# A sliding-window attention and MLP kernel: rows of maxima sent by ScalarE, and four of six feature blocks made 512 tokens at a time

## The chip, the cores and the metric

One NeuronCore of a Trainium2 chip runs the whole kernel; the others are idle. The metric is the device time of one execution in microseconds, the median of several runs. A profiled execution gives the trace that the profile is made from. The engines are named as the profile names them: PE is TensorE, ACT ScalarE, DVE VectorE, POOL GpSimd, SP SyncE.

## The reference

2048 tokens of 640 features are layer-normalised. One branch is attention with 32 heads of 20 features over a window of 256 tokens; the other is an MLP with 1536 hidden features and a squared ReLU. The output gates one with the other.

```python
xn = _layernorm(x)
# attention, H = 32, Dh = 20, W = 256
qkv = (xn @ wqkv).reshape(B, S, 3, H, Dh)
scores = einsum("bhqd,bhkd->bhqk", q, k) * Dh ** -0.5
scores = where(0 <= q_index - k_index < W, scores, -1e9)
s = (softmax(scores) @ v).reshape(B, S, D) @ wo
# MLP, D = 640, F = 1536
h = xn @ w1 + b1
r = where(h > 0, h, 0)
g = silu((r * r) @ w2 + b2)
out = x + s * g
```

## The kernel before

**Precision.** Each large product is made three times: an operand is split into a high part (rounded) and a low part (the rest), and high x high, high x low and low x high are added up in PSUM. ACT makes the high part, DVE or POOL subtracts it to get the low part. So one feature block of the first MLP half, with 5 chunks of 128 input features, takes 15 products.

**Half products.** The fillers below run each product as two halves of 64 contraction rows (`half`, L466). The front half of a job runs in one stream, its back half some time later in a second stream (`ahead`, `behind`, `backlog`), and the two streams alternate on PE, so that two halves of different jobs are on the array together. PE takes its instructions strictly in the order in which they were written: a product that waits for something holds both streams.

**Stages.** A first stage (to about 116 us) normalises, transposes and makes V and the first group of Q and K. A last one (from about 804 us) multiplies by `wo` and gates. Between them run 267 steps of attention, one query block of 128 tokens of a pair of heads each, and between the instructions of each step `fill` puts filler work: the other groups of Q and K (`qkps`), then the MLP, in eight blocks: two halves of the hidden features (`hf`), each over four blocks of 512 tokens (`b`).

**A step of attention.** `scores` writes the scores of one query block (`sps`), `maxima` takes their row maxima on DVE. Nine steps later (`LAG`) `scores_t` makes the transposed scores (`stps`), with two more contraction rows: ones on one side, the negative maxima (high and low part) on the other. `exps` takes the exponential on ACT into `p`, POOL cuts the window's corners, and `values` multiplies by V once in four steps (`ops`). One pair of banks holds `stps`, so the next `scores_t` waits until the exponential has read the last one.

Every fourth step `max_rows` (L488) turns the maxima of four query blocks: PE transposes, ACT negates and copies (`row`, L499), ACT rounds (`mrow`, L500), POOL subtracts (L501), and two DMAs (L503) on SP's queue bring the two rows, 4 KB each, into the two spare rows of `qs`. The `stps` that reads them first comes three steps after they are issued.

**A block of the MLP** (L891 on). Its first half makes hidden features: the loop `for th in range(2): for fp in range(NFH // 2)` (L912) goes over two token halves of 256 and three pairs of feature blocks, six accumulations. Each (`Acc`, one of three PSUM banks of 512 columns) holds two feature blocks of the same 256 tokens, 30 products of 256 columns. Its evacuation has two passes, `part(0)` and `part(1)`, one for each feature block: ACT `relu` and `hh` (the square, rounded), DVE `sq` (the exact square), POOL `hl` (the low part). The second pass is put 0.8 us of planned time later by `later`; when its POOL instruction is written, the accumulation counts as `made` and its bank as free 1.0 us on.

The second half makes 4 token tiles (`tt`) x 2 output halves (`nh`), jobs of 18 products of 320 columns (`yps`), three for each of six feature blocks (`fc`); their weights are slices of `hh` and `hl`. A product waits in the plan, `while (tt // 2, fc // 2) not in made`, and tiles 0 and 1 need only the accumulations of the first token half.

**What sets the order.** The order is written out ahead of time by this planner (`COST`, `pace`, `later`, `room`), engine by engine; on the chip only the waits on semaphores move it.

Of the kernel before, what the change touches and what calls it, by code (L numbers as in the profile page):

```python
# [9 lines left out]
F32 = mybir.dt.float32  # L10
# [19 lines left out]
HP = P // 2  # L30
HALF = D // 2
NFH = F // 2 // P
FHALF = F // 2
MT = 256
LAG = 9
# [17 lines left out]
def f32(ap):  # L53
    return ap.bitcast(F32)
# [3 lines left out]
def attn_mlp_kernel(ctx: ExitStack, tc, x, wqkv, wo, w1, b1, w2, b2, out):  # L58
# [429 lines left out]
    def max_rows(p, g, tps):  # L488
        i = p % 2

        def one(j):
            r = slice(j * HP, (j + 1) * HP)
            nc.tensor.transpose(tps[:HP, j, 3 * P:3 * P + HP], mts[g % 2][r, :], ident[r, r])
        both(lambda: one(0), lambda: one(1), COST[P])

        def rest():
            row = at2.tile([8, P], F32, tag="row", bufs=1, name="row")
            mrow = at2.tile([8, 2, P], F32R, tag="mrow", bufs=1, name="mrow")
            nc.scalar.activation(row.rearrange("m (j n) -> m j n", j=2), tps[:8, :, 3 * P:3 * P + HP], AF.Copy, scale=-1.0)  # L499
            nc.scalar.activation(mrow[:, 0, :], row, AF.Copy)  # L500
            nc.gpsimd.tensor_sub(mrow[:, 1, :], row, f32(mrow[:, 0, :]))  # L501
            for a in range(2):
                nc.sync.dma_start(f32(qs[i])[KR + a:KR + a + HP + 1:HP, g * BT:(g + 1) * BT].rearrange("h (q n) -> h q n", q=4), f32(mrow)[:, a, :])  # L503
        return rest

    pts = {}
# [319 lines left out]
    def filler():  # L826
# [64 lines left out]
        for n, (hf, b) in enumerate(blocks):  # L891
# [13 lines left out]
            def used(n=n, b=b, nxt=nxt):  # L905
# [3 lines left out]
                    shut.discard("o")  # L909
                if n < last and blocks[n + 1][1] != b:  # L910
                    nxt.extend(load_xb(blocks[n + 1][1]))
            for th in range(2):  # L912
                for fp in range(NFH // 2):
                    yield from room()
                    ps = Acc(BT, "hps")

                    def evac(ps=ps, th=th, fp=fp, fi=hf * NFH + 2 * fp, hs=hs, made=made):
                        hh = [stg.tile([P, BT], F32R, tag="stg", name="hh"),
                              stg.tile([P, BT], F32R, tag="stg", name="hl") if fp == 0 else wgt.tile([P, D], F32R, tag=f"wg{'kq'[fp % 2]}l", name="hl")[:, :BT]]
                        hs[th, fp] = hh  # L920

                        def part(i):
                            vload[0] += 0.5
                            sl = slice(i * MT, (i + 1) * MT)
                            r = at2.tile([P, MT], F32, tag="relu", name="relu")
                            nc.scalar.activation(r, ps.tile[:, sl], AF.Relu, bias=b1t[:, fi + i:fi + i + 1])  # L926
                            nc.scalar.activation(hh[0][:, sl], r, AF.Square)

                            def rest():
                                sq = at2.tile([P, MT], F32, tag="sq", name="sq")  # L930
                                nc.vector.scalar_tensor_tensor(sq, ps.tile[:, sl], b1t[:, fi + i:fi + i + 1], r, ALU.add, ALU.mult)  # L931
                                nc.gpsimd.tensor_sub(hh[1][:, sl], sq, f32(hh[0][:, sl]))  # L932
                                if i:
                                    made.add((th, fp))
                                    ps.free(1.0)
                            later(0.7, rest)
                        part(0)
                        later(0.8, lambda: part(1))
                    job = open_job(evac, *([used] if (th, fp) == (1, NFH // 2 - 1) else []))
                    mms = [(i, lin1(wt1, (wp * KC + c) * FHALF + (2 * fp + i) * P, P), xb[xp][:, c * BT + th * MT:c * BT + (th + 1) * MT]) for i in range(2) for c in range(KC) for wp, xp in ((0, 0), (0, 1), (1, 0))]  # L940
                    for m, (i, w_, x_) in enumerate(mms):
                        halves(job, ps, w_, x_, m == 0, m == len(mms) - 1, i * MT, MT)
                        yield 0.1065
            if n % NB == 0:
                ensure(f"2{hf}")
            if n == NB:
# [3 lines left out]
            for tt in range(4):  # L950
                t = b * 4 + tt
                place = [None]
                jobs = []

                def start(nh, hf=hf, t=t, place=place, idx=4 * (n - NB) + tt, end=n == NB - 1 and tt == 3, n=n, tt=tt):
                    sl = slice(nh * HALF, (nh + 1) * HALF)
                    ps = Acc(HALF, "yps")

                    def evac():
                        vload[0] += 0.5  # L960
                        if not nh:
# [12 lines left out]

                def product(jb, nh, fc):
                    ps, job, _ = jb
                    while (tt // 2, fc // 2) not in made:
                        if state[2] < 10 ** 6:
                            yield None
                        elif tasks:  # L980
                            finish()
                        else:
                            drain(backlog, 1)
                    for hp, wp in ((0, 0), (0, 1), (1, 0)):
                        jb[2] += 1
                        halves(job, ps, hs[tt // 2, fc // 2][hp][:, fc % 2 * MT + tt % 2 * P:fc % 2 * MT + (tt % 2 + 1) * P], lin1(wt2, (wp * NFH + fc) * D + nh * HALF, HALF), jb[2] == 1, jb[2] == 3 * NFH)
# [117 lines left out]
    whole = [False]  # L1104
    fl = filler()
    steps = NP * NT + LAG + PLAG
    pace = (8 * (KC - 1) * 15 * COST[BT] + 4 * NB * (3 * 30 * COST[MT] + 4 * 18 * COST[HALF]) + NP * (2 * NT * COST[3 * P] + NB * PV)) / (steps - 1)

    def fill(upto):
        soon()  # L1110
# [89 lines left out]
```

## Time and profile before

| what | value |
|---|---|
| median of 3 runs | 885.0 us (881.82 to 885.83) |
| the profiled execution | 882.05 us, of which the traced span is 880.3 |
| granted TensorE clock, mean | 0.999 |
| DVE, ACT, POOL busy | 57%, 47%, 37% of the span |
| data moved | 168.59 MB, mean 192 GB/s |

The profile gives the busy time of each engine, the waits ("who waited for whom", total, times and longest), and the chain of work that ended last, followed back from the end. A group line gives engine, operation, output and inputs by the program's names, shapes, count, then busy time, the mean of one in ns, and the idle time before them. A line of the timeline gives the start and the length in us. "64*128" is the number of contraction rows and output columns of the array that a product uses. Matmuls overlap each other, so the length of one (283 ns) is not what it costs; the distance between two is.

### The profile page before, as it was taken

To read this page: it belongs to the slowest core of one execution; us is meant where nothing else is said; L and a number is where in the kernel's file an instruction comes from. 1 tells how busy PE (TensorE), PEld (TensorE's weight loads), DVE (VectorE), ACT (ScalarE), POOL (GpSimd) and SP (SyncE) were. 2 spreads that over 40 slices of the span, in tenths; PEclk is the share of its full clock that TensorE was granted. 3 is DMA by queue.
4 is the path that set the end of the run, shared out by engine and by line. 5 is a ranking of instruction groups with operands and counts; after the bars stand their busy time and mean duration, and the time that the engine had idled before them with its cause. 6 is when DMAs were issued, how large, how long until landed. Compare 5 with 4: busy or idle time off the path is not lost.

```text
span 880.3 us, 26692 instructions
## 1 busy us (share of the span) xinstructions
PE 860.6 (98%) x10640; PEld 802.6 (91%) x10640; DVE 498.7 (57%) x1448; ACT 414.8 (47%) x800; POOL 329.9 (37%) x700
## 2 busy tenths in 40 slices
PE   8999999999999999999999999999999999999997
PEld 8999999888888899989989989988998989989997
DVE  7652146656567755555555676754655555354774
ACT  5222114545556744744644664743653654642231
POOL 6010002333333643534633543643543543621343
PEclk9999999999999999999999999999999999999999
DMA  7997687778788363263366255475255364165995
GB/s 269 313 394 265 179 230 256 229 249 278 240 269 297 84 223 108 60 224 96 95 207 174 73 154 145 130 223 150 76 202 161 90 209 119 52 196 183 284 299 175
DMA packets 85988, 168.59 MB, mean 192 GB/s; under 512 B 8680, under 2 KB 40552, under 8 KB 83304
## 3 DMA queue, kind: packets, MB, share of 16 engines
q1 hardware_dynamic: 85864, 166.89, 60.1%
q8 instruction: 84, 1.38, 0.7%
q14 instruction: 40, 0.33, 0.1%
HBM read 94.71 MB, written 71.57 MB: 189 GB/s over the span
## 4 chain that ended last, share of the span: by engine, by line
PE 76%; DMA 11%; ACT 4%; DVE 4%; issue 3%; POOL 2%; SPq 0%; DVEq 0%; POOLq 0%; ACTq 0%
PE yps L468 16%; PE hps L468 16%; PE qkps L468 13%; PE ops L546 8%; PE vps L228 8%; DMA qs<-mrow 5%; PE stps L518 4%; PE sps L478 4%; PE qkps L205 3%; DMA out_dram<-res 3%; POOL res L1099 2%; PE wops L599 1%; DMA ks<-k_d 1%; ACT p L524 1%; ACT relu L926 1%
## 5 line engine op out<-in xcount | busy, mean ns | idle before, releaser
L486 DVE CUSTOM_DVE_ANT_0 junk<-sps,mask 128x384 bf16<-128x384 f32 (+2 forms) x512 | 271.9, 531 | 205.0 <-PE sps L478 75.1
L524 ACT ACTIVATE p<-stps 128x768 f32<-128x768 f32 (+2 forms) x256 | 196.9, 769 | 258.0 <-PE stps L518 202.1
L468 PE MATMUL yps<-w,hh 64*128 64x320 f32 x1536 | 231.6, 310 | 4.0 <-DVE sq L931 3.0
L525 POOL TENSOR_SCALAR_AFFINE_SELECT p<-p 128x256 f32<-128x256 f32 x256 | 104.6, 409 | 332.7 <-ACT p L524 327.6
L468 PE MATMUL hps<-xb,w 64*128 64x256 f32 x2520 | 218.2, 283 | 0.0
L468 PEld LDWEIGHTS hps<-xb,w 64*128 64x128 f32 x2520 | 206.4, 187 | 5.2 <-issue 5.1
L468 PEld LDWEIGHTS yps<-w,hh 64*128 64x128 f32 x1536 | 188.8, 185 | 9.7 <-DVE sq L931 4.8
L468 PE MATMUL yps<-w,hl 64*128 64x320 f32 x768 | 182.8, 309 | 0.0
L478 PE MATMUL sps<-ks,qs 60*128 60x384 f32 (+2 forms) x512 | 139.9, 344 | 1.9 <-DVE mt L486 1.6
L518 PE MATMUL stps<-qs,ks 62*128 62x384 f32 (+2 forms) x512 | 130.1, 335 | 5.8 <-DMA qs<-mrow 5.7
L468 PEld LDWEIGHTS yps<-w,hl 64*128 64x128 f32 x768 | 121.6, 185 | 2.1 <-issue 2.1
L468 PE MATMUL qkps<-xT,wgkh 64*128 64x512 f32 x320 | 100.9, 395 | 0.0
L468 PE MATMUL qkps<-xT,wgqh 64*128 64x512 f32 x320 | 99.4, 393 | 0.0
L546 PE MATMUL ops<-p,vp 128*21 128x128 f32 (+1 forms) x2112 | 92.8, 313 | 0.0
L527 POOL TENSOR_SCALAR_AFFINE_SELECT p<-p 128x256 f32<-128x256 f32 x224 | 92.1, 411 | 0.0
L518 PEld LDWEIGHTS stps<-qs,ks 62*128 62x128 f32 x512 | 83.4, 187 | 8.7 <-issue 7.7
L478 PEld LDWEIGHTS sps<-ks,qs 60*128 60x128 f32 x512 | 84.4, 185 | 5.1 <-DVE mt L486 3.9
L546 PEld LDWEIGHTS ops<-p,vp 128*21 128x21 f32 x2112 | 65.2, 100 | 22.3 <-issue 8.8
L932 POOL TENSOR_TENSOR hl<-sq,hh 128x256 fp32r<-128x256 f32 x96 | 70.6, 736 | 27.5 <-DVE sq L931 22.9
L228 PE MATMUL vps<-wv,xT 128*128 128x320 f32 x480 | 71.5, 308 | 0.0
L228 PEld LDWEIGHTS vps<-wv,xT 128*128 128x128 f32 x480 | 70.5, 188 | 0.1
L931 DVE SCALAR_TENSOR_TENSOR sq<-hps,b1t,relu 128x256 f32<-128x256 f32 x96 | 46.2, 482 | 39.2 <-ACT relu L926 39.1
(100 smaller groups left out, 1212.1 us busy)
## 6 DMA issues: line engine op xcount, KB each, us to landing
ks<-k_d SPq DMA_DIRECT2D x64, 240.0 KB
qs<-q_d SPq DMA_DIRECT2D x64, 240.0 KB
xb<-xs SPq DMA_DIRECT2D x12, 1280.0 KB
xs<-xT SPq DMA_DIRECT2D x8, 1280.0 KB
y<-ysb SPq DMA_DIRECT2D x32, 320.0 KB
k_d<-shm SPq DMA_DIRECT2D x19, 512.0 KB
q_d<-shm SPq DMA_DIRECT2D x19, 512.0 KB
o<-osb SPq DMA_DIRECT2D x64, 128.0 KB
```

The source lines that it names most:

```text
L205: nc.tensor.matmul(ps, wt[:, c, :], xT[part][b][:, c * BT + t0:c * BT + t0 + n], start=m == 1, stop=m == 3 * KC)
L228: nc.tensor.matmul(ps, xT[xp][b][:, c * BT + t * P: c * BT + (t + 1) * P], wv[wp][:, c, nh * HALF:(nh + 1) * HALF], start=first and m == 0 ...
L468: return nc.tensor.matmul(out, a[r], b_[r], skip_group_check=True, **kw)
L478: nc.tensor.matmul(ss[hh][:, :nk], qs[i][o, q * P:(q + 1) * P], ks[i][o, k0 * P:k0 * P + nk], start=True, stop=True)
L486: nc.vector.tensor_tensor_reduce(out=junk[:, :nk], in0=ss[hh][:, :nk], in1=mask[:, 3 * P - nk:], scale=1.0, scalar=-3.0e38, op0=ALU.add, o ...
L518: nc.tensor.matmul(tps[:, hh, :n], ks[i][o, kb * P:(kb + 1) * P], qs[i][o, kb * P:kb * P + n], start=True, stop=True)
L524: nc.scalar.activation(p32[:, :, :n], tps[:, :, :n], AF.Exp, scale=SCALE)
L525: nc.gpsimd.affine_select(p32[:, :, 0:P], p32[:, :, 0:P], pattern=[[0, 2], [1, P]], compare_op=ALU.is_ge, fill=0.0, base=0, channel_multip ...
L527: nc.gpsimd.affine_select(p32[:, :, 2 * P:], p32[:, :, 2 * P:], pattern=[[0, 2], [-1, P]], compare_op=ALU.is_gt, fill=0.0, base=0, channel ...
L546: nc.tensor.matmul(ot[r0:r0 + VW, c0:c0 + len(part), :], vps[p][:, kb // 4, kb % 4, hh, :], pt[:, hh, :].rearrange("p (t n) -> p t n", n=P ...
L931: nc.vector.scalar_tensor_tensor(sq, ps.tile[:, sl], b1t[:, fi + i:fi + i + 1], r, ALU.add, ALU.mult)
L932: nc.gpsimd.tensor_sub(hh[1][:, sl], sq, f32(hh[0][:, sl]))
```

## The change

Two things. `max_rows` issues its two DMAs on ScalarE's queue instead of SP's, the first at once, the second 0.8 us of planned time later. And the first half of an MLP block makes feature blocks 0 to 3 (`WIDE = NFH - 2`) with all 512 tokens, one block to a bank, 15 products of 512 columns and one evacuation of 512 columns; blocks 4 and 5 stay as before: two accumulations, one for each token half, with two blocks of 256 tokens. The second half finds its slices accordingly, and `pace` follows from the new costs.

```diff
@@ max_rows
-            for a in range(2):
-                nc.sync.dma_start(f32(qs[i])[KR + a:KR + a + HP + 1:HP, g * BT:(g + 1) * BT].rearrange("h (q n) -> h q n", q=4), f32(mrow)[:, a, :])
+            def send(a):
+                nc.scalar.dma_start(f32(qs[i])[KR + a:KR + a + HP + 1:HP, g * BT:(g + 1) * BT].rearrange("h (q n) -> h q n", q=4), f32(mrow)[:, a, :])
+            send(0)
+            later(0.8, lambda: send(1))
@@ filler, first half of a block
-            for th in range(2):
-                for fp in range(NFH // 2):
-                    ps = Acc(BT, "hps")
+            for u in range(NFH):
+                ps = Acc(BT, "hps")
+                th = u - WIDE
+                cols = [(u, 0, BT)] if th < 0 else [(WIDE + i, th * MT, MT) for i in range(2)]
...
-                            later(0.7, rest)
-                        part(0)
-                        later(0.8, lambda: part(1))
+                        later(0.7, rest)
+                    part(0)
+                    if len(cols) > 1:
+                        later(0.8, lambda: part(1))
...
-                    mms = [(i, lin1(wt1, (wp * KC + c) * FHALF + (2 * fp + i) * P, P), xb[xp][:, c * BT + th * MT:c * BT + (th + 1) * MT]) for i in range(2) for c in range(KC) for wp, xp in ((0, 0), (0, 1), (1, 0))]
+                mms = [(i, lin1(wt1, (wp * KC + c) * FHALF + fc * P, P), xb[xp][:, c * BT + t0:c * BT + t0 + n_]) for i, (fc, t0, n_) in enumerate(cols) for c in range(KC) for wp, xp in ((0, 0), (0, 1), (1, 0))]
@@ second half of a block
-                    while (tt // 2, fc // 2) not in made:
+                    u = fc if fc < WIDE else WIDE + tt // 2
+                    o = tt * P if fc < WIDE else (fc - WIDE) * MT + tt % 2 * P
+                    while u not in made:
```

Two places of the written order. The first is PE's order in the fourth MLP block, at the end of the first `yps` job (its 13th to 18th products) while the sixth accumulation's back half runs beside it. "waits" names the engine whose semaphore the instruction stands for. Before, where the weights `hh_8552` and `hl_8553` are the third accumulation's:

```order
L468 MATMUL yps_8781<-w2_0_1_3933,hh_8552 128x320
L468 MATMUL hps_8673<-xb0_2_7524,w1_0_1_3364 128x256
L468 MATMUL yps_8781<-w2_0_2_4087,hh_8552 128x320
L468 MATMUL hps_8673<-xb0_2_7524,w1_0_0_3362 128x256
L468 MATMUL yps_8781<-w2_0_1_3933,hl_8553 128x320
L468 MATMUL hps_8673<-xb1_2_7525,w1_0_0_3362 128x256
L468 MATMUL yps_8894<-w2_0_0_3931,hh_8284 128x320 [waits DVE_49]
```

With the change, where `hh_8268` and `hl_8269` are the fifth accumulation's:

```order
L469 MATMUL yps_8262<-w2_0_1_3878,hh_8268 128x320 [waits Activation_49]
L469 MATMUL hps_8121<-xb0_2_7133,w1_0_1_3356 128x256
L469 MATMUL yps_8262<-w2_0_2_4007,hh_8268 128x320
L469 MATMUL hps_8121<-xb1_2_7134,w1_0_1_3356 128x256
L469 MATMUL yps_8262<-w2_0_1_3878,hl_8269 128x320 [waits Pool_49]
L469 MATMUL hps_8121<-xb0_2_7133,w1_0_2_3490 128x256
L469 MATMUL yps_8262<-w2_0_1_3878,hh_8268 128x320 [waits Activation_49]
L469 MATMUL hps_8121<-xb0_2_7133,w1_0_0_3354 128x256
L469 MATMUL yps_8262<-w2_0_2_4007,hh_8268 128x320
L469 MATMUL hps_8121<-xb1_2_7134,w1_0_0_3354 128x256
L469 MATMUL hps_8121<-xb0_2_7133,w1_0_1_3356 128x256
L469 MATMUL yps_8262<-w2_0_1_3878,hl_8269 128x320 [waits Pool_49]
```

The same products stand there, but they now wait for the two passes of the accumulation that was finished last.

The second place is ACT's order at the same point: the exponential (`p32`), the rows of maxima, and the two evacuation passes of the fifth accumulation (`hps_8525` before, `hps_8025` after). Before:

```order
L524 ACTIVATE p32_8815<-stps_8808 128x768
L551 ACTIVATE osb_8819<-ops_1358 128x256
L926 ACTIVATE relu_8824<-hps_8525,b1t_108 128x256
L927 ACTIVATE hh_8822<-relu_8824 128x256
L926 ACTIVATE relu_8842<-hps_8525,b1t_108 128x256
L927 ACTIVATE hh_8822<-relu_8842 128x256
L524 ACTIVATE p32_8878<-stps_8869 128x768
L499 ACTIVATE row_8882<-stps_8869 8x128
L500 ACTIVATE mrow_8883<-row_8882 8x128
```

With the change:

```order
L528 ACTIVATE p32_8249<-stps_8240 128x768
L500 ACTIVATE row_8253<-stps_8240 8x128
L501 ACTIVATE mrow_8254<-row_8253 8x128
L505 DMA qs1_1350<-mrow_8254 2x4x128
L933 ACTIVATE relu_8270<-hps_8025,b1t_108 128x256
L934 ACTIVATE hh_8268<-relu_8270 128x256
L505 DMA qs1_1350<-mrow_8254 2x4x128
L933 ACTIVATE relu_8291<-hps_8025,b1t_108 128x256
L934 ACTIVATE hh_8268<-relu_8291 128x256
L528 ACTIVATE p32_8315<-stps_8308 128x768
```

The two DMA issues are new on ACT; here one stands ahead of the first pass and one between the two passes.

More of the change, by code (lines that the diff above doesn't have):

```diff
@@ L32 @@
 NFH = F // 2 // P
+WIDE = NFH - 2
 FHALF = F // 2
@@ L911, in used @@
                     nxt.extend(load_xb(blocks[n + 1][1]))
-            for th in range(2):
-                for fp in range(NFH // 2):
-                    yield from room()
-                    ps = Acc(BT, "hps")
[L917 to L935, printed above, removed]
-                            later(0.7, rest)
-                        part(0)
-                        later(0.8, lambda: part(1))
-                    job = open_job(evac, *([used] if (th, fp) == (1, NFH // 2 - 1) else []))
-                    mms = [(i, lin1(wt1, (wp * KC + c) * FHALF + (2 * fp + i) * P, P), xb[xp][:, c * BT + th * MT:c * BT + (th + 1) * MT]) for i in range(2) for c in range(KC) for wp, xp in ((0, 0), (0, 1), (1, 0))]
-                    for m, (i, w_, x_) in enumerate(mms):
-                        halves(job, ps, w_, x_, m == 0, m == len(mms) - 1, i * MT, MT)
-                        yield 0.1065
@@ L985, in product @@
                         jb[2] += 1
-                        halves(job, ps, hs[tt // 2, fc // 2][hp][:, fc % 2 * MT + tt % 2 * P:fc % 2 * MT + (tt % 2 + 1) * P], lin1(wt2, (wp * NFH + fc) * D + nh * HALF, HALF), jb[2] == 1, jb[2] == 3 * NFH)
+                        halves(job, ps, hs[u][hp][:, o:o + P], lin1(wt2, (wp * NFH + fc) * D + nh * HALF, HALF), jb[2] == 1, jb[2] == 3 * NFH)
                         yield 0.133
```

26 lines of the change are left out of this document (25 added, 1 removed).

## The prediction

> **What bounds the kernel now.** First the page: the span, the engines, the chain by line.
>
> ```profile
> span 880.3 us, 26692 instructions
> PE 860.6 (98%) x10640; PEld 802.6 (91%) x10640; DVE 498.7 (57%) x1448; ACT 414.8 (47%) x800; POOL 329.9 (37%) x700
> q1 hardware_dynamic: 85864, 166.89, 60.1%
> ```
>
> TensorE (PE) is busy nearly throughout, so time goes only if PE needs less for its products or stands still less. ScalarE (ACT) is free half of the time. All transfers share one queue, which keeps the 16 DMA engines busy for 60% of the span. Next the view of waits, to see for what PE stands still and what SyncE's queue is held by:
>
> ```profile
> PE stps L518 <- DMA qs<-mrow: 5.7, 8, 1.7
> PE yps L468 <- DVE sq L931: 3.0, 6, 0.7
> SPq L503 <- ACT mrow L500: 66.2, 42, 3.2
> ACT p L524 <- PE stps L518: 202.1, 154, 4.0
> ```
>
> Two waits of PE matter here: eight times the transposed scores (`stps`) stand for the row of maxima that a DMA brings (5.7 us), and six times a second-half product (`yps`) stands for a bank that VectorE's `sq` still reads (3.0 us). ACT mostly waits for PE. Last the chain in order of time, for the pace of products that follow each other:
>
> ```profile
> 121.83 2.07 PE qkps L468 x18
> 131.37 2.31 PE qkps L468 x20
> 356.89 2.02 PE hps L468 x34
> 364.27 1.96 PE hps L468 x31
> 487.53 2.04 PE hps L468 x32
> 10.82 1.79 PE qkps L205 x15
> 38.51 6.87 PE qkps L205 x30
> ```
>
> The first two are half products (64 rows) with 512 columns, 4.38 us for 38, 115 ns each; the next three are the first MLP half with 256 columns, 6.02 us for 97, 62 ns each. The last two are full products: 119 ns with 256 columns, 229 ns with 512.
>
> **Part 1: 512 tokens a product.** The counts, by form:
>
> ```profile
> L468 PE MATMUL hps<-xb,w 64*128 64x256 f32 x2520 | 218.2, 283 | 0.0
> L468 PE MATMUL hps<-xT,w 64*128 64x256 f32 x360 | 31.8, 283 | 0.0
> L851 ACT ACTIVATE shm<-qkps 128x512 fp32r<-128x512 f32 x32 | 19.0, 593 | 15.0 <-PE qkps L468 14.6
> L854 DVE TENSOR_TENSOR slo<-qkps,shm 128x512 fp32r<-128x512 f32 x32 | 22.0, 688 | 7.6 <-ACT shm L851 7.6
> L926 ACT ACTIVATE relu<-hps,b1t 128x256 f32<-128x256 f32 x96 | 45.2, 470 | 24.4 <-DVE sq L931 18.6 <-PE hps L468 5.6
> L927 ACT ACTIVATE hh<-relu 128x256 fp32r<-128x256 f32 x96 | 40.1, 418 | 3.1
> L931 DVE SCALAR_TENSOR_TENSOR sq<-hps,b1t,relu 128x256 f32<-128x256 f32 x96 | 46.2, 482 | 39.2 <-ACT relu L926 39.1
> ```
>
> Of the 2880 half products, two thirds (1920) become 960 with 512 columns; the columns streamed stay the same. Two of 256 cost 124 ns, one of 512 costs 115: 9 ns x 960 = 8.6 us less. The bounds: the fastest of the rows (59.4 ns) gives 3.4 us, the slowest (63.8) 11.8 us, the full products 2 x 119 - 229 = 9 ns x 480 = 4.5 us. I take 7.5 us, between the full products and the mean of the halves, as PE is the bound where they run. The page "TensorE: Matmul & The Clock Gate" of the Trainium skill, section "Back-to-back issue gap", gives a fixed part of about 2.5 ns to a matmul in isolation; by it 480 fewer full-width starts would save an estimated 1.2 us. The rows show about four times that fixed part, and they decide.
>
> The evacuations get fewer and longer: 128 ACT passes of 256 (0.47 and 0.42 us in the rows) become 64 of 512 (0.59 us by the copy of that size), one `sq` of 0.69 us stands for two. That frees some 19 us of ACT and 9 us of VectorE; both lie under PE's products and I cost them at nothing, except at the place of part 3.
>
> **Part 2: the rows go by ScalarE.** SP no longer issues these 128 DMAs, and its later transfers no longer stand behind the wait of 66.2 us. The rows themselves no longer stand in line behind what SP has issued. The long landings in the chain, the cost of an issue, and a transfer into an empty queue:
>
> ```profile
> 386.45 6.16 DMA qs<-mrow
> 589.18 6.42 DMA qs<-mrow
> 0.80 2.83 DMA xt<-in_A_x_dram
> L503 SPq DMA_DIRECT2D qs<-mrow x128: 495/508/1685, 127.3 to 760.4; - x128
> ```
>
> A row of 4 KB that takes 6.2 us is standing behind megabytes; 320 KB into empty queues landed in 2.8 us. If the second queue is served in turn with the first, the rows land in at most that time and all eight waits go: 5.7 us, plus the run-out of the matmul ahead at each (about 0.3 us of a latency of 0.28 to 0.36), 8 us at most. I take 7.0; the other bound is nothing. Here the page "DMA: Bandwidth & Descriptors" of the Trainium skill says two things. Its section "Queues, rings and completion order" has each DMA engine go round its queues packet by packet, which is the 7 us. Its section "Issuing engines are not separate DMA queues" says that issuing from several engines saves only sequencer time, which would be 0. No row of before has a second queue, so it stays a rival below.
>
> What it costs is ACT time: 128 x 0.508 = 65 us on a queue that is in order. One such place:
>
> ```profile
> 374.59 0.31 ACT L500 ACTIVATE mrow<-row 8x128 fp32r<-8x128 f32 x1
> 375.04 0.45 POOL L501 TENSOR_TENSOR mrow<-row,mrow 8x128 fp32r<-8x128 f32 x1
> 374.93 1.11 SPq L503 DMA_DIRECT2D qs<-mrow  x2
> 376.41 0.82 ACT L524 ACTIVATE p<-stps 128x768 f32<-128x768 f32 x1
> 378.82 0.81 ACT L524 ACTIVATE p<-stps 128x768 f32<-128x768 f32 x1 [1.59 <-PE stps L518]
> ```
>
> After `mrow` (374.90) the first issue takes 0.5 us; the second waits for GpSimd's part (375.49), then 0.5 us: ACT is held for 1.1 to 1.3 us. Behind it stand an evacuation and the exponential of 376.41, which frees the one pair of banks that PE's next `stps` needs. It would end near 377.7; PE comes at about 378.5. The 1.59 us of idle time behind it take the push up. Laying 1.3 us on each of the 64 groups (both issues together, each following row pushed until idle time takes it up), 49 cost PE nothing and 15, nearly all beside first-half evacuations, 7.2 us in sum. The wider evacuations and the second issue put 0.8 later thin this out: I take 2.0 us, bounds 0 and 7.2.
>
> **Part 3: a wait that the new split brings.** Before, the first second-half job (tokens 0 to 127) read blocks made long ago. Now its 13th to 18th products read feature blocks 4 and 5 of the fifth accumulation, whose evacuation is only then running: the order above shows four waits there, on Activation and Pool, where none stood. The same place in the trace of before (fourth block):
>
> ```profile
> 503.73 0.42 ACT L927 ACTIVATE hh<-relu 128x256 fp32r<-128x256 f32 x1
> 504.43 0.73 POOL L932 TENSOR_TENSOR hl<-sq,hh 128x256 fp32r<-128x256 f32 x1 [0.54 <-DVE sq L931]
> 504.83 0.42 ACT L927 ACTIVATE hh<-relu 128x256 fp32r<-128x256 f32 x1
> 505.52 0.74 POOL L932 TENSOR_TENSOR hl<-sq,hh 128x256 fp32r<-128x256 f32 x1 [0.36 <-DVE sq L931]
> 503.29 0.31 PE L468 MATMUL yps<-w,hh 64*128 64x320 f32 x1
> 503.58 0.31 PE L468 MATMUL yps<-w,hl 64*128 64x320 f32 x1
> 504.12 0.39 PE L468 MATMUL yps<-w,hh 64*128 64x320 f32 x1
> 504.50 0.30 PE L468 MATMUL yps<-w,hl 64*128 64x320 f32 x1
> 505.44 0.41 PE L468 MATMUL yps<-w,hh 64*128 64x320 f32 x1 [0.49 <-DVE sq L931]
> ```
>
> The 13th, 15th, 16th and 18th product start at 503.29, 503.58, 504.12 and 504.50. High part, low part, high and low part of the fifth accumulation end at 504.15, 505.16, 505.25 and 506.26. If the products had to wait for these, PE would stand 0.9 us, then until 505.16, and the 18th would start 1.8 us late. PE is in order, so both of its streams stop. In exchange the wait of 505.44 (0.5 us, for an earlier step of the same evacuation) is over by then. The same comparison at the other seven blocks gives 2.0, 0.3, 2.4, 1.2, 2.3, 1.8 and 2.1 us, 14 us in all. The planner holds these products back until the last pass is issued, which, counted by the products that stand between in both orders, puts them 1.4 us later at two blocks and 0.7 at one, and about where they were at the others: I take 10.5 us gross, and 7.5 us net of the 3.0 us of `yps` on `sq`. In three blocks a DMA issue also stands between the two passes on ACT. Bounds: 0 net, and 13 (14 and three times 0.6, less 3).
>
> **The sum.** -7.5 (products) - 7.0 (rows) + 2.0 (ACT held) + 7.5 (fifth block) = -5.0 us. The profiled execution itself took 882.05 us, 1.75 more than its span; it goes to 877. It lies 2.95 us under the median of the three runs (885.0), so the median goes to 880.0.
>
> **Rivals.** (a) The new wait is hidden: the planner's delay and the shorter chain of passes suffice, nothing net for part 3: -12.5 us, 872.5. For it speaks that `made` gates those products; against it that the gate opens when the low part is issued, and the low part ends a VectorE and a GpSimd pass later (0.48 and 0.74 us).
> (b) ScalarE's queue decides, slower: the issues stand ahead of the passes for which PE now waits, so that parts 2 and 3 come to their upper ends, 13 + 7.2 us, with 1.3 us more for the held groups beside them: +21.5 - 14.5 = +7, 892. It decides from the point where both together pass 14.5 us. For it: 0.5 us an issue and the row `SPq L503 <- ACT mrow` show real holds; against it: ACT's 202 us of waiting for PE.
> (c) The second queue brings the rows no sooner, because the engines are full and not the queue: part 2 gains nothing, +2.0 us, 887. For it: the 60% share of the engines; against it: 4 KB need hardly any of their time.
>
> **How the numbers follow.** Forecast 45%, (a) 22%, (b) 20%, (c) 13%. This kernel's runs tell 0.5% (4.4 us) from no change: faster is below 880.6, slower above 889.4. The forecast, with its own range of 875 to 886, gives 27% faster and 18% the same; (a) is faster; (b) slower; (c) splits 9 to 4. Faster 49%, same 27%, slower 24%. The range goes from short of the full gains of (a) with the upper bound on the products, 868, to (b), 892.
>
> **What would show it.** Right: runs of `hps` in the chain near 115 ns a product; no wait of `stps` for `mrow`; a second hardware queue; new PE waits of `yps` on ACT `hh` and GpSimd `hl`, 7 to 13 us in sum, at eight places. The forecast is wrong if those waits stay under 4 us (a), if PE waits for ACT's exponentials or VectorE's maxima for more than 5 us in addition (b), or if `stps` goes on waiting for `mrow` (c).

## The result, and the profile after

| | before | after |
|---|---|---|
| median, us | 884.5 (881.82 to 885.83, 4 runs) | 923.5 (917.79 to 924.6, 4 runs) |
| ratio, 95% interval | 1 | 1.0432 [1.0382, 1.0482] |
| profiled execution, and its span | 882.05, 880.3 | 923.47, 921.7 |
| granted TensorE clock, mean | 0.999 | 0.990 |

The change made the kernel 39 us slower. The page of the changed kernel, in the order in which that of before was read: busy times, queues, and the chain by line ("..." stands for lines left out).

```profile
PE 876.9 (95%) x9680; PEld 794.0 (86%) x9680; DVE 489.8 (53%) x1416; ACT 403.7 (44%) x736; POOL 324.0 (35%) x668
...
q1 hardware_dynamic: 84584, 166.36, 57.8%
...
q10 hardware_dynamic: 1280, 0.53, 0.2%
...
PE yps L469 15%; PE hps L469 12%; PE qkps L469 11%; DMA qs<-mrow 8%; PE vps L229 8%; PE ops L550 7%; PE stps L522 4%; PE sps L479 4%; PE qkps L206 3%; DMA out_dram<-res 2%; PE wops L603 2%; ACT relu L933 2%; POOL res L1109 1%; ACTq L505 1%;
```

PE went from 98% busy to 95%: it stands still more, 44.8 us of the span instead of 19.7. That is 25 of the 41 us that the span grew by; the other 16 are busy time, part of it at a lower clock (last section). There is a second hardware queue now (q10), so the rows do go their own way. ACT computes less than before (403.7 us against 414.8), and yet it takes more of the chain (6% against 4%). Issuing a DMA is not counted as busy, so the page's busy time hides it. The waits of PE, in the columns total, times, longest:

```profile
PE stps L522 <- DMA qs<-mrow: 11.0, 14, 2.1
PE yps L469 <- POOL hl L939: 9.8, 11, 1.6
PE yps L469 <- DVE ysb L972: 5.0, 2, 3.8
PE yps L469 <- DVE sq L938: 3.8, 4, 1.3
...
PE sps L479 <- DVE mt L487: 2.4, 9, 0.4
...
PE yps L469 <- ACT hh L934: 1.2, 2, 0.6
```

The wait for the rows, which was to vanish, doubled (5.7 us before). The waits for `hl` and `hh` are the ones forecast, 11.0 us together. The wait for `ysb`, two of 5.0 us in all, was not. The view of one tile, `mrow`, says who waited for it. Before, it listed GpSimd and PE alone. Now:

```profile
...
  PE stps L522: 11.0, 14
  ACT p L528: 10.7, 7
  ACT relu L933: 6.2, 9
  ACT w L769: 3.6, 6
...
```

Ahead of the exponential `p`, the evacuation `relu` and the split of weights `w`, ACT now computed nothing until an issue that itself waits for `mrow` was through. A piece of the timeline of the changed kernel shows how that reaches PE (start, length, engine, line, instruction; in brackets the idle time before it and what ended it):

```profile
520.38 0.31 ACT L501 ACTIVATE mrow<-row 8x128 fp32r<-8x128 f32 x1
...
520.72 0.52 ACTq L505 DMA_DIRECT2D qs<-mrow  x1
...
521.34 0.47 ACT L933 ACTIVATE relu<-hps,b1t 128x256 f32<-128x256 f32 x1 [0.65 <-ACT mrow L501]
...
521.85 0.52 ACTq L505 DMA_DIRECT2D qs<-mrow  x1
521.91 0.48 DVE L938 SCALAR_TENSOR_TENSOR sq<-hps,b1t,relu 128x256 f32<-128x256 f32 x1 [1.53 <-ACT relu L933]
...
522.31 0.41 PE L469 MATMUL yps<-w,hh 64*128 64x320 f32 x1 [0.61 <-ACT hh L934]
...
522.31 0.55 DVE L487 CUSTOM_DVE_ANT_0 junk<-sps,mask 128x384 bf16<-128x384 f32 x1
...
523.32 0.41 PE L469 MATMUL yps<-w,hl 64*128 64x320 f32 x1 [0.45 <-POOL hl L939]
```

The first issue keeps ACT for 0.65 us. `relu` is late by that, `sq` on DVE stood 1.53 us for `relu`, the row maxima of the next scores (`junk`) stand behind `sq`, and PE waits first for `hh`, then for `hl`. One held slot is paid by three engines that work strictly in order.

### The profile page after: what moved, and what is told of

It is laid out like the page before. It is cut to its first block, busy times and chain, and to the rows that moved or that the text cites. A ratio compares the mean times of both kernels' runs of the same rounds, so it can differ in the third digit from the quotient of the medians.

```text
span 921.7 us, 24567 instructions
## 1 busy us (share of the span) xinstructions
PE 876.9 (95%) x9680; PEld 794.0 (86%) x9680; DVE 489.8 (53%) x1416; ACT 403.7 (44%) x736; POOL 324.0 (35%) x668
## 4 chain that ended last, share of the span: by engine, by line
PE 67%; DMA 12%; ACT 6%; issue 5%; DVE 4%; POOL 3%; ACTq 1%; SPq 0%; DVEq 0%; POOLq 0%
PE yps L469 15%; PE hps L469 12%; PE qkps L469 11%; DMA qs<-mrow 8%; PE vps L229 8%; PE ops L550 7%; PE stps L522 4%; PE sps L479 4%; PE qkps L206 3%; DMA out_dram<-res 2%; PE wops L603 2%; ACT relu L933 2%; POOL res L1109 1%; ACTq L505 1%; ACT p L528 1%
## 5 line engine op out<-in xcount | busy, mean ns | idle before, releaser
L469 PE MATMUL hps<-xb,w 64*128 64x512 f32 (+1 forms) x1680 | 216.2, 342 | 0.1
L469 PEld LDWEIGHTS hps<-xb,w 64*128 64x128 f32 x1680 | 177.2, 188 | 11.9 <-issue 4.9
L479 PE MATMUL sps<-ks,qs 60*128 60x384 f32 (+2 forms) x512 | 137.2, 347 | 2.5 <-DVE mt L487 2.4
L522 PE MATMUL stps<-qs,ks 62*128 62x384 f32 (+2 forms) x512 | 123.5, 343 | 13.4 <-DMA qs<-mrow 11.0
L469 PEld LDWEIGHTS yps<-w,hl 64*128 64x128 f32 x768 | 119.8, 189 | 14.8 <-POOL hl L939 12.8
L522 PEld LDWEIGHTS stps<-qs,ks 62*128 62x128 f32 x512 | 76.4, 188 | 21.1 <-issue 15.7
L479 PEld LDWEIGHTS sps<-ks,qs 60*128 60x128 f32 x512 | 79.4, 186 | 9.0 <-DVE mt L487 7.2
L939 POOL TENSOR_TENSOR hl<-sq,hh 128x512 fp32r<-128x512 f32 (+1 forms) x64 | 65.4, 1023 | 27.5 <-DVE sq L938 24.1
L938 DVE SCALAR_TENSOR_TENSOR sq<-hps,b1t,relu 128x512 f32<-128x512 f32 (+1 forms) x64 | 39.4, 615 | 52.4 <-ACT relu L933 52.3
```

Source lines behind the costliest of these rows:

```text
L469: return nc.tensor.matmul(out, a[r], b_[r], skip_group_check=True, **kw)
L479: nc.tensor.matmul(ss[hh][:, :nk], qs[i][o, q * P:(q + 1) * P], ks[i][o, k0 * P:k0 * P + nk], start=True, stop=True)
L522: nc.tensor.matmul(tps[:, hh, :n], ks[i][o, kb * P:(kb + 1) * P], qs[i][o, kb * P:kb * P + n], start=True, stop=True)
L938: nc.vector.scalar_tensor_tensor(sq, ps.tile[:, sl], bias, r, ALU.add, ALU.mult)
```

## The experiments

Two theories to begin with. A: the loss comes from the split of the first MLP half and its new waits. B: it comes from the DMAs that ScalarE issues. Eleven variants ran. Medians and ratios are against the kernel before, run beside them (884.2 us beside the runs 1, 2, 3 and 8 of the headings below, 884.9 beside 4, 5, 9 and 10, 884.4 beside 6 and 11, 883.5 beside 7).

### 1 and 2. One part at a time

The kernel before with only the rows on ScalarE:

```diff
-                nc.sync.dma_start(<row a of qs>, f32(mrow)[:, a, :])
+            def send(a):
+                nc.scalar.dma_start(<row a of qs>, f32(mrow)[:, a, :])
+            send(0)
+            later(0.8, lambda: send(1))
```

> The kernel before with the rows of maxima sent by ScalarE alone, no 512-token products. If the new waits of the MLP split are the loss (theory A), this costs 0 to 8 us (885 to 893) and the MLP split the rest. If ScalarE's issues are the loss (theory B: the engine is held, or the second queue lands the rows later), it costs 20 us or more (905 to 925). By the prediction on record it would gain 5 us (880).

Measured: 912.8 us, 1.0312 [1.0282, 1.0342].

The changed kernel with `max_rows` as before, that is the split alone:

> The changed kernel with the rows on SyncE's queue again, so the 512-token blocks alone. Theory A: 905 to 920, with waits of the second-half products on GpSimd's low parts of 8 us or more and a granted clock below 1. Theory B: 875 to 885, those waits under 4 us. If the two parts only hurt together, both this and the run with the rows alone stay within 6 us of 885.

Measured: 895.9 us, 1.0126 [1.0079, 1.0173], between the ranges of the two theories. The parts add up: 28.6 + 11.7 = 40.3 against 39.0 together. So B carries most of it and A the rest. PE's waits for the rows and for `sq` in the run with the rows alone:

```profile
PE stps L521 <- DMA qs<-mrow: 10.8, 10, 2.8
PE yps L468 <- DVE sq L934: 7.0, 10, 1.5
PE sps L478 <- DVE mt L486: 3.6, 11, 1.0
```

All three are longer than before (5.7, 3.0 and 1.6 us): the rows come later, and so do the evacuations and the maxima. The line of the maxima in the kernel before, and that of a wait that matters further down:

```profile
PE sps L478 <- DVE mt L486: 1.6, 5, 0.8
PE yps L468 <- DVE ysb L964: 0.9, 2, 0.7
```

The written order of PE, DVE and GpSimd is the same as before in this run, instruction by instruction. Only ACT's and SP's queues differ, by these DMAs.

### 3 to 6. ScalarE's time against the second queue's landing

First, rows on SP as before, and ScalarE issues two 4 KB stores to a scratch tensor at the change's places:

```diff
+            def send(a):
+                nc.scalar.dma_start(scr_d[a], f32(mrow)[:, a, :])
+            send(0)
+            later(0.8, lambda: send(1))
```

> The kernel before, rows still on SyncE's queue, but ScalarE issues two transfers of the same size at the same places into a scratch buffer that nobody reads. If holding ScalarE is what costs, this equals the run with the rows on ScalarE within 3 us. If the landing in the second queue is what costs, this stays within 3 us of 885 while the other is slower. Adds a store of 8 KB per group that the kernel does not need.

Measured: 901.4 us, 1.0184 [1.0151, 1.0217]: neither of the two outcomes, but a loss of 17.2 us. These issues were shorter than those of the rows (minimum/median/maximum in ns):

```profile
L507 ACTq DMA_DIRECT2D scr<-mrow x128: 269/270/1692, 128.8 to 778.2; - x128
```

and the rows' own, in run 1:

```profile
L504 ACTq DMA_DIRECT2D qs<-mrow x128: 503/518/1687, 127.4 to 791.7; - x128
```

By that the stores would hold ScalarE half as long, but the second of each group also waits for GpSimd's half of `mrow`. Counted in the traces from the end of the instruction or issue ahead on ACT to the end of the issue, the 128 stores take 64.9 us and the 128 issues of rows in run 1 take 73.6. The next run takes DMAs out of it: rows on SP, and ScalarE makes two copies that nobody reads.

```diff
+            def busy(a):
+                idle = at2.tile([8, 5, P], BF16, tag="idle", bufs=1, name="idle")
+                nc.scalar.activation(idle, f32(mrow)[:, a:a + 1, :].to_broadcast([8, 5, P]), AF.Copy)
+            busy(0)
+            later(0.8, lambda: busy(1))
```

> The kernel before, whose rows stay in SP's queue. In each of the 64 groups ScalarE makes two copies of a row of maxima into a tile that nobody reads, 640 elements a partition, at the two places where the changed kernel issues its DMAs (the second after GpSimd's half of mrow). By the rows of before a 640-element copy takes about 0.73 us and overlaps its neighbours by about 0.1, so that ScalarE's slot is about as long as the 0.65 us that the issue of a row of maxima took from it. In the run with two dummy stores the issue was only 0.27 us long, so that run held ScalarE about half as long as the change does. Theory 'ScalarE's time alone': the loss grows with the time held, so this run costs what the rows on ScalarE cost, 22 to 34 us: 906 to 918 us. Rival 'time plus landing': the time held costs the 17 us of the dummy stores and the rest is the second queue's landing: 897 to 905 us. Rival 'DMA issues alone hurt': 884 to 890 us.

Measured: 903.3 us, 1.0204 [1.0172, 1.0236], inside the range of the rival "time plus landing". Its copies as a group (busy time, mean ns of one, idle time before), and PE's waits:

```profile
L507 ACT ACTIVATE idle<-mrow 8x640 bf16<-8x640 f32 x128 | 94.0, 734 | 6.2 <-POOL mrow L501 0.5
```

```profile
PE yps L468 <- DVE sq L937: 7.5, 10, 1.6
PE stps L524 <- DMA qs<-mrow: 5.4, 8, 1.7
PE sps L478 <- DVE mt L486: 3.5, 10, 1.0
PE hps L468 <- DVE sq L937: 2.0, 4, 0.5
```

No row has moved and no DMA was added, and the waits for `sq` and `mt` are as long as with the rows on ScalarE, while the wait for the rows is that of before. Two more instructions a group on ACT alone therefore cost 18.4 us. Counted as above they hold it for 98.1 us, less about 0.09 us each by which the next instruction overlaps them, so some 86 us: not less than the issues. The other 10 of the 28.6 us are a difference between two runs. The waits of `stps` for the rows are 5 to 6 us longer in run 1 than in the kernel before (10.8 us, and 1.2 that the profile can't assign, against 5.7). And its granted clock was 0.993 or 0.994 in the median against 0.998 here, by which I estimate 4 us of 912.

Then one row on each queue: the first on ScalarE, and in a further run the second.

```diff
-                nc.sync.dma_start(<row a of qs>, f32(mrow)[:, a, :])
+                q = (nc.scalar, nc.sync)[a]
+                q.dma_start(<row a of qs>, f32(mrow)[:, a, :])
```

> The kernel before with the first row of each group (the rounded part) sent by ScalarE, the second (GpSimd's part) still by SP. ScalarE is held half as long as in the change's rows and never waits for GpSimd. Theory 'ScalarE's time alone', in proportion: half of 28.6, about 14 us, 895 to 902 us. Rival 'the wait for GpSimd at the second issue is what costs': 884 to 889 us. Rival 'the second queue's landing costs the most': the group is not complete before the row in that queue, 11 us or more, and PE's waits for mrow's rows are as long as with both rows there (about 10.8 us in the profile, against 5.7 before).

```diff
-            for a in range(2):
-                nc.sync.dma_start(<row a of qs>, f32(mrow)[:, a, :])
+            send(0, nc.sync)
+            later(0.8, lambda: send(1, nc.scalar))
```

> The kernel before with the first row of each group (the rounded part) left in SP's queue and the second (GpSimd's part) sent by ScalarE at the changed kernel's place. ScalarE is held once a group, as in the run with the first row alone on ScalarE (893.9 us, +9.0). Theory 'time held, and a landing term that comes from the late second row': the held time costs about 9 again, and PE's waits for the rows rise from 5.7 us before (2.6 with only the first row on ScalarE) towards the 10.8 us of both rows there, so 896 to 901 us. Rival 'time held alone': as with the first row, 891 to 896 us, waits for the rows within 2 us of before. Rival 'two rows in one queue are what lands late': waits for the rows stay below those of before, 888 to 895 us.

Measured: 893.9 us, 1.0100 [1.0064, 1.0135], and 894.3 us, 1.0114 [1.0079, 1.0149]. The wait for the rows, in this order:

```profile
PE stps L519 <- DMA qs<-mrow: 2.6, 4, 0.8
...
PE stps L519 <- issue: 1.6, 1, 1.6
```

```profile
PE stps L521 <- DMA qs<-mrow: 3.6, 5, 1.8
...
PE stps L521 <- issue: 2.4, 3, 1.0
```

Half the issues cost about half of the 18.4 us (9.0 and 9.9), the first run a little less than its theory's range (895 to 902), the second inside that of "time held alone". The first had up to 3.1 us back from shorter waits for the rows. Which of the two rows ScalarE sends, and so whether it waits for GpSimd, makes no difference that can be told.

The length of the hold does not rank the runs: counted as above, 36.2 us cost 9.0, 66.0 (the second row, with the wait for GpSimd) cost 9.9, 64.9 (the stores) cost 17.2 and some 86 (the copies) cost 18.4. The number of instructions added to a group does: one costs 9 to 10 us, two 17 to 18 (in run 1 the late landing comes on top). Copies of another length were not tried, so how the cost depends on length stays open.

The landing term that I expected from the late second row did not show: the row of waits for `mrow` fell below before's in both runs (with the 1.6 and 2.4 us that the profile can't assign they are 4.2 and 6.0, so the second is about level with it). Spread over SP's and ScalarE's queues PE waits no longer for the rows than before. With both in ScalarE's queue it does. The packets of that queue can be told apart in the trace: the last one of a row comes 3.4 us after the end of `mrow` (median of 64) with the first row alone there, and 4.1 us for the first and 4.8 us for the second row with both. Most of that passes before the first packet. In run 1 it starts 0.64 us after the end of the issue at the three places where SP's queue kept the DMA engines less than 10% busy meanwhile, and 3.2 to 3.8 us after it (medians) where SP's queue kept them over 40% busy. So a queue of its own did not bring the rows past SP's transfers.

### 7. The landing without ScalarE

The second row sent by GpSimd, right behind the subtraction that makes it:

```diff
-            for a in range(2):
-                nc.sync.dma_start(<row a of qs>, f32(mrow)[:, a, :])
+            send(0, nc.sync)
+            send(1, nc.gpsimd)
```

> The kernel before with the second row of each group sent by GpSimd, which makes it, right behind its subtraction; the first stays in SP's queue and ScalarE sends nothing. Theory 'the loss is ScalarE's time, and two queues land the rows sooner': PE's waits for the rows fall from 5.7 us to about the 2.6 to 3.6 us of the runs with one row on ScalarE, nothing is paid on ScalarE, 880 to 885 us. Rival 'any engine between the products and the next stage costs as much when it is held': GpSimd's selects and hl come later, 888 to 896 us. Rival 'GpSimd's queue lands later than SP's': PE's waits for the rows rise over 7 us, 886 to 892 us.

Measured: 891.3 us, 1.0102 [1.0069, 1.0135], inside the ranges of both rivals. The waits decide for the one on landing.

```profile
qs<-mrow POOLq DMA_DIRECT2D x64, 4.0 KB, 4.3
```

```profile
PE stps L521 <- DMA qs<-mrow: 6.2, 6, 2.4
PE stps L521 <- issue: 4.6, 5, 1.6
PE yps L468 <- DVE sq L934: 2.4, 5, 0.6
...
PE sps L478 <- DVE mt L486: 1.5, 4, 0.8
```

The first line is the view of DMAs: 4.3 us from issue to landing. The waits for `sq` and `mt` are no longer than before, and PE waits for no work of GpSimd, so no harm of holding GpSimd for 64 issues shows; the wait of `stps` is about 5 us longer (the row without a releaser taken with it). Here late rows cost 7.7 us with ScalarE untouched. It is another queue than ScalarE's, so it shows what such lateness costs, not why ScalarE's queue has it.

The semaphore counts in the traces date the landings. The table has the median time from the end of `mrow` until both rows of a group have landed, beside PE's waits for them (with those that the profile can't assign):

| who sends the rows | both landed after, us | PE's waits, us |
|---|---|---|
| SP both (before) | 4.3 | 5.7 |
| ScalarE the first, SP the second | 4.3 | 4.2 |
| SP the first, ScalarE the second | 4.8 | 6.0 |
| ScalarE both (run 1) | 5.2 | 12.0 |
| SP the first, GpSimd the second | 5.3 | 10.8 |

The long waits go with the late pairs.

### 8 to 10. Where the split loses

In the profile of the split alone the new wait stands as forecast, and a second one was not:

```profile
PE yps L469 <- POOL hl L936: 9.3, 10, 1.6
...
PE yps L469 <- DVE ysb L969: 4.6, 2, 2.9
```

To take the first away, the products that need the fifth accumulation are written later in the first token tile:

```diff
-                    job = start(nh)
-                    for fc in range(NFH):
-                        yield from product(job, nh, fc)
+                    opened.append(start(nh))
+                    for fc in range(NFH if tt else WIDE):
+                        yield from product(opened[nh], nh, fc)
+                if not tt:
+                    for nh in range(2):
+                        for fc in range(WIDE, NFH):
+                            yield from product(opened[nh], nh, fc)
```

> 512-token blocks, rows on SyncE, and in the first token tile of each second half the products of feature blocks 4 and 5 come after blocks 0 to 3 of both output halves, so the fifth accumulation is needed 12 products later (about 1.8 us of PE time or more). Theory A: 8 us or more faster than the 512-token blocks without this, waits of second-half products on low parts under 4 us. Theory B: within 3 us of it.

Measured: 888.8 us, 1.0050 [1.0034, 1.0066], 7.1 us less than the split alone, a little short of theory A's 8. The wait for `hl` is gone from the list. What remains is at the end of the MLP:

```profile
PE yps L469 <- DVE ysb L969: 8.0, 2, 6.5
```

The timeline of the split alone shows the cause there, on ACT and then on DVE:

```profile
783.50 0.72 ACT L774 ACTIVATE wo<-raw 128x640 fp32r<-128x640 f32 x1
...
797.40 0.74 ACT L774 ACTIVATE wo4h<-raw 128x640 fp32r<-128x640 f32 x1 [2.22 <-DMA raw<-in_A_wo_dram]
```

```profile
798.18 0.82 DVE L775 TENSOR_TENSOR wo4l<-raw,wo4h 128x640 fp32r<-128x640 f32 x1 [1.87 <-ACT wo4h L774]
798.92 0.95 DVE L1047 TENSOR_TENSOR ob<-ob,sums 128x768 f32<-128x768 f32 x1
...
801.65 0.88 DVE L969 TENSOR_TENSOR ysb<-yps,yin 128x320 f32<-128x320 f32 x2
```

The pieces of `wo` are split in order as they arrive. Before, the first and the last (`wo4h`) were:

```profile
776.27 0.74 ACT L773 ACTIVATE wo<-raw 128x640 fp32r<-128x640 f32 x1
...
785.22 0.73 ACT L773 ACTIVATE wo4h<-raw 128x640 fp32r<-128x640 f32 x1
```

In the split the last comes after a wait for its load, 9.9 us after attention's last product (`ops`) instead of 1.2 us. DVE then works off `wo4l`, `ob` and `oT` ahead of `ysb`, and PE has no free bank until then. The planner lets the pieces go one by one after the last first-half product has been written: before, three went out before the end of attention, with the split only one. Letting them go without that spacing:

```diff
-        gap = {"1": 2, "2": 2, "o": 2}.get(tag[0], 1) + (tag == "10") - (vload[0] < 0.4 and tag[0] != "g")
+        gap = {"1": 2, "2": 2, "o": 1}.get(tag[0], 1) + (tag == "10") - (vload[0] < 0.4 and tag[0] != "g")
-        if vload[0] > 0.6 and vload[1] < {"2": 1, "g": 2 * (tag != "g4")}.get(tag[0], 2):
+        if vload[0] > 0.6 and vload[1] < {"2": 1, "o": 0, "g": 2 * (tag != "g4")}.get(tag[0], 2):
```

on the split alone,

> The 512-token split with the rows in SP's queue, and the first pieces of wo are let go as soon as the last first-half product is out (no pause for the vector engines, one step apart instead of two), three pieces before the end of attention as in the kernel before instead of one. Theory 'the split's loss is the late load of wo': it takes back 7 to 9 of the 11.7 us, 886 to 889 us, and PE's waits at 770 to 813 us for ysb and for the last raw loads go. Rival 'the new wait for the fifth accumulation's hh and hl is the loss': 893 to 897 us, as without it.

and together with the later products:

> The same release of wo, with the products of the blocks 4 and 5 after those of 0 to 3 of both halves of the columns in the first tile of each second half, rows in SP's queue. Theory 'late wo and new wait together are the whole loss, and the split itself gains': below the kernel before, 878 to 882 us. Rival 'the split gains nothing by itself': 884 to 889 us.

Measured: 892.1 us, 1.0088 [1.0056, 1.0120], and 882.2 us, 0.9970 [0.9947, 0.9993]. The first took back 3.8 us, less than the 7 to 9 expected, and its interval overlaps that of the split alone, so on that base the mend is not settled; but its wait for `ysb` went from 4.6 us to 1.0. The second is clear: 888.8 to 882.2 us, intervals apart. In its last stretch (770 to 815 us) PE waits for `ysb` once, for 1.3 us.

The new wait is worth the distance between the two runs with the early `wo`: 892.1 - 882.2 = 9.9 us. And with both mended the split gains, 2.7 us. That variant is the only one that beats both kernels, by 0.3% against the kernel before. The kernel before with the early `wo` alone did not run, so part of the 2.7 us may be the early `wo`'s and not the split's.

### 11. The whole change, mended

The change with both mends of the split, the rows still on ScalarE:

> The whole change (rows on ScalarE, 512-token split) with the two mends of the split: the products of the blocks 4 and 5 after those of 0 to 3 of both halves of the columns in the first tile of each second half, and the early release of wo. Theory 'the two parts add': the split is worth about -2.7 us and the rows on ScalarE +28.6, 907 to 914 us. Rival 'with room left by the mends the rows on ScalarE cost less': 890 to 904 us. Rival 'the new waits hid part of the rows' cost': above 916 us.

Measured: 908.7 us, 1.0272 [1.0244, 1.0301]. The mends take 14.8 us from the change, 13.7 from the split alone; the rows on ScalarE cost 27.1 us on the mended split (24.3 above the kernel before, instead of 2.7 below it), 28.6 on the kernel before. The parts add to within 1.5 us in every combination tried, and what is left of the change's loss is the rows.

## Why the prediction was wrong, step by step

The forecast was 880, with a range of 868 to 892; it came to 923.5.

| term | forecast, us | measured, us | from |
|---|---|---|---|
| 512-token products | -7.5 | -2.7, the mended split | run 10 against before |
| the fifth block's new wait | +7.5 net | +9.9 | run 9 against run 10 |
| late `wo` | not seen | +3.8 to +6.6 | 2 against 9, 8 against 10 |
| rows land sooner | -7.0 | about +10 | 1 against 4 |
| ScalarE held | +2.0, at most 7.2 | +18.4 | run 4 against before |
| sum | -5.0 | 39.4, by the smaller value for `wo` | measured as a whole: 39.0 |

The measured terms are differences of medians, each good to some 3 us, so the closeness of the two sums is in part luck.

**The step that failed most is the cost of ScalarE's held time.** The replay over the rows of before asked when each following exponential of ScalarE would end and whether PE came later. It took ACT's idle time as cover, and ACT has plenty: 47% busy. But that idle time lies elsewhere, behind waits for PE. Where a group of rows is sent, an evacuation or an exponential is often ready and stands behind the issue (7 + 9 + 6 times for `p`, `relu` and `w` in the `mrow` rows of after). And the replay stopped at ACT: it had no price for `sq` on DVE and the maxima queued behind it. With the copies on ACT, PE's waits for `sq` and `mt` rose from 4.6 to 13.0 us, including 2.0 for first-half products that wait for a bank. These are 8.4 of the 18.4 us; the others I can't assign wait by wait. Counted over the whole trace, the distances of 0.3 us or more between the starts of successive products sum to 29.1 us (47 of them) before and 47.1 us (69) with the copies.

**The landing had the wrong sign.** The 6.2 us landings were put down to a queue full of megabytes, and the new queue was to be served in turn, with landings of 2.8 us at most. The failed step is that bound: with both rows in the new queue the first lands 4.5 us after its issue in the median (4.1 before) and the pair 5.2 us after `mrow` (4.3 before), and the waits went from 5.7 to 10.8 us. The rival that expected no gain from a second queue (887) was nearer, and its sign came (`stps` goes on waiting for `mrow`), but it too left out a loss. The Trainium skill's page "DMA: Bandwidth & Descriptors" says in "Issuing engines are not separate DMA queues" that the second engine saves only the sequencer's time, usually small beside the DMA. By that the 7 us were not there to gain, and the run with both rows there bears this out; but here the sequencer's time was ACT's, and that was the larger price. The same page of the Trainium skill has in "Queues, rings and completion order" the rule of turns, packet by packet, by which the -7.0 was argued. No trace here shows the turns themselves. What the forecast drew from them, rows that pass the bulk, did not come: 3.2 to 3.8 us to the first packet while SP's queue is busy, against 0.64 us while it is idle.

**The fifth block's wait was right**, in place, releaser and size: `yps` on `hl`, 9.3 us in ten waits in the split alone, 9.8 in the change, and gone when the products are written later. The 3.0 us of `yps` on `sq` that were to go in exchange did not: 2.6 us of them stayed in the split alone, 3.8 in the change.

**The products themselves cost what was forecast.** Where three first-half products of one size follow each other, the mean distance of their starts is 62.0 ns before with 256 columns and 116.4 ns in the mended split with 512, against 62 and 115 in the forecast: 960 x (2 x 62.0 - 116.4) = 7.3 us. The time shows 2.7. Part of the rest is known: PE's waits of `yps` for `sq` and `ysb` rose from 3.0 and 0.9 us to 5.4 and 2.8. The remainder is open.

**Not seen at all:** that the planner's pieces of `wo` hang on the step in which the last first-half product is written, and that standing still can also cost clock (below).

Rival (b), ScalarE's queue decides, had the mechanism and the sign of the change. The waits by which it was to be known, PE's for exponentials and maxima, stayed under its 5 us in the changed kernel (2.2 us, and 2.4 against 1.6): the delay reached PE through `sq`, `hh` and `hl`. The rival stopped at 892 because it kept the landing gain and the bound of 7.2 us of the same replay.

## What to carry to other kernels

An engine that is idle half of the time is not free at a given place: before a DMA or any other work is put on its queue, look at what is ready behind that place, and follow it through each engine that works in order, not only to the next row of the engine itself. A dummy copy at the same place measures that price without moving a DMA. And where a planner lets work go at "the step in which X was written", a change of X moves that work too, so compare its place at the end of the program as well as at the change.

## What the runs showed of the hardware

**The clock fell after stalls shorter than its own stretch, in three of four places.** The kernel before ran at a mean granted clock of 0.999. In the changed kernel it fell to half four times, in stretches of 3.4 or 6.8 us, 17 us in all: at 460, 525, 740 and 832 us. The windows of the changed kernel, with the columns length, busy PE, PEld, DVE, ACT, POOL (instructions), clock, DMA share, GB/s:

```profile
456.40:459.90 3.50, 2.21 (x23) 1.94 (x21) 1.44 (x4) 2.62 (x6) 2.04 (x5) 1.00 0.95 334
459.90:463.30 3.40, 3.40 (x28) 3.40 (x27) 1.63 (x6) 0.56 (x2) 1.12 (x3) 0.51 0.99 404
...
514.60:518.00 3.40, 2.26 (x36) 1.83 (x28) 1.45 (x5) 0.83 (x2) 1.67 (x3) 1.00 0.05 19
...
521.40:524.80 3.40, 1.60 (x15) 0.83 (x11) 1.92 (x6) 2.42 (x5) 1.45 (x4) 1.00 0.14 43
524.80:531.60 6.80, 5.97 (x54) 5.17 (x58) 1.53 (x5) 2.32 (x4) 1.54 (x4) 0.50 0.00 0
```

and of the 3.4 us ahead of the last drop:

```profile
828.60:832.00 3.40, 0.00 (x0) 0.00 (x0) 2.49 (x4) 1.84 (x2) 0.00 (x0) 1.00 0.20 73
```

PE was busy for 2.21 of 3.5 us before the first drop, in the half-clock stretch all the time, with fewer products (28 in 3.4 us). Before the second it was busy for 1.60 of 3.4. But 2.26 of 3.4 at 514.6 was followed by full clock, so the share alone doesn't tell. Nor does the longest stall: one of 2.1 us that ended at 730.9 was followed by full clock too. Ahead of the fourth drop PE stood for 3.8 us, the wait for `ysb`. The page "TensorE: Matmul & The Clock Gate" of the Trainium skill, in "Part 1: The HAM clock gate", gives windows of 3413 ns that run free of the kernel and a drop after an idle one. The length agrees, and so does the fourth drop. For the other three an idle window was not needed: the longest stall in the 3.4 us ahead of each was 1.3, 1.6 and 1.6 us long, the second of them still running when the clock fell.

What it costs shows between executions of one kernel: the changed one took 917.8 us at a mean clock of 0.994 and 923.5 to 924.6 at 0.989 to 0.990. Clock times time says that about 9 of its 923.5 us were lost that way, against some 2 of the kernel before. These 7 us are not a further term: they are inside the terms above, since the variants' times hold their own loss of clock. It differs: the rows on ScalarE ran at 0.992 to 0.994, the copies, which stall too, at 0.996 to 0.998.

**The issue of a DMA has no fixed length.** The same 4 KB took ACT 518 ns into the rows of `qs` and 270 ns into a contiguous scratch tensor. What in the destination makes the difference was not tried. Why two rows in ScalarE's queue land later than one in each was not tried either; both stay open.
